# Pooled attention and SiLU network on one core: an exponential set aside, a filler and a last quarter reordered, query transposes moved ahead of value sums, eight more dummy matmuls

## The chip, the cores and the metric

The kernel runs on one core of one Trainium2 chip. The metric is the device time of one execution in microseconds (us). Four runs of the kernel before took 290.15, 290.22, 291.45 and 291.74 us, with a median of 290.83 us.

The engines are named as in the profile. PE is TensorE doing matmuls, PEld is its weight load, DVE is VectorE, ACT is ScalarE, POOL is GpSimd and SP is SyncE. A small q behind a name (SPq, POOLq) is the engine's sequencer, which issues the DMAs.

## The reference

There are 8 batches of 8 heads, with 576 queries, keys and values of 64 numbers each. Keys and values are averaged over groups of 8 (576 to 72), and the attention output of all heads becomes the input of a two-layer network with SiLU.

```python
k_p = k.reshape(B, H, Sp, 8, D).mean(axis=3)        # 576 -> 72 rows
v_p = v.reshape(B, H, Sp, 8, D).mean(axis=3)
scores = q @ k_p.transpose(0, 1, 3, 2) / sqrt(D)
attn = exp(scores) / sum(exp(scores))               # the maximum is subtracted first
x = (attn @ v_p).transpose(0, 2, 1, 3).reshape(4608, 512)
h = x @ w_in                                        # 512 -> 2048
out = (h * sigmoid(h)) @ w_out                      # 2048 -> 512, float32
```

## The kernel before

The 4608 tokens are cut into 9 tiles of 512 (the loop over t, L785). Each tile has an upward product (`up`, L471: x times w_in, SiLU into h_T) and a downward one (`down`, L571, for t = 0, and `down_quarters`, L638, for all others: h times w_out, then the stores). Tiles t >= 1 compute part of both products with sums of matrix quarters (x_sum, h_sum, w_sum), which DVE makes, so that PE has fewer matmuls. The attention of batch t+1 is woven into the two products of tile t.

The weaving is written by hand. Each product has a list of fillers, pairs of a step number and a call; a generator `spread` (L417) yields one step before each matmul and, once a step is past, makes the calls due by then. The order of all instructions on every engine follows the program text, and each engine runs its own in that order. PSUM tiles come from two pools, `mm` with 3 banks and `at` with 5 (L89), and a new tile waits until the reader of an old one is done.

The attention of a batch runs through these steps, each of them one helper. `slot_sums` (L269, DVE) adds the rows of k or v in groups. `select_k` and `select_v` (L289, L305, PE) pick the sums into kz_ps and v_ps. `copy_k` and `copy_v` (L302, L319, on ACT or DVE) bring them to SBUF as kz and vp. `q_transpose` (L150, DVE, one call for half a group of four heads) makes qT. `scores` (L343, PE) makes four tiles sc_ps and ACT takes the exponential of each into es (L359). `denominators` (L363) sums es on PE and ACT (or DVE by a reciprocal, L375) inverts it into rec. `numerators` (L382) multiplies es with vp on PE (nu_ps, L395), and DVE multiplies by rec into xT (L404).

Batch 0 has no tile to be woven into. Its attention is the prologue, written out at L735 to L767, in four parts: `part(g, f)` is head group g, half f of the queries. Between its steps stand dummy matmuls, `warm_up(n)` (L698), n products of 128x512 on zeros whose result is not read; there are 37 in all. In the middle of it all `attn_tables` and `moe_tables` (L410, L413) switch ACT between the function tables for exponential and for SiLU. `up` of tile 0 follows the last `warm_up`; its first matmuls read xT of parts (0,0) and (1,0), and the parts (0,1) and (1,1) end as fillers of it.

Tile 0's `down` runs three output blocks m = 0, 1, 2 together over all 16 slices g of h_T (48 steps), copies each to o_sb (ACT for 0 and 2, DVE for 1) and then runs m = 3 alone, whose PSUM tile is a bank that m = 0 held. Fillers among these steps:

```python
    f_down.append((37 + 3 * j, lambda j=j: select_v(1, j, "at")))    # L836
    sc_at, den_at, nu_at = (1, 16, 30), (16, 30, 44), (44, 55, 56)    # L874
```

Tile 1 does the attention of batch 2. Its four query transposes have the steps `[24, 25, 26, 8]` (L829); the first three are fillers of `up`, the fourth one of `down_quarters`. There, step 8 also has both calls of `slot_sums("v")` (L843), which are earlier in the list. The second third of the scores, at step 31, is the first reader of the fourth transpose.

From tile 1 on, the fillers load batch t+2: `load_q` on POOL's queue, `load_one` on SP's, `load_rest` on POOL's again (L864 to L868).

Of the kernel before, what the change touches and what calls it, by code (L numbers as in the profile page):

```python
# [36 lines left out]
def kernel(  # L37
# [9 lines left out]
    nc = tc.nc  # L47
# [5 lines left out]
    d_model = H * D  # L53
    d_ff = moe_w_in.shape[1]
    KF = d_model // 128
    KG = d_ff // 128
# [44 lines left out]
    w_out_sb = singles.tile([128, KG, d_model], BF16, name="w_out_sb")  # L101
# [167 lines left out]
    def slot_sums(name, j, halves=False):  # L269
        raw = row_tiles[name][j]  # L270
        dst = rows5[name][:, SA:] if j else rows5[name][:, :SA]
        w = RE // 4 if halves else RE // 2
        while w > D:
            nc.vector.tensor_add(  # L274
                out=raw[..., :w], in0=raw[..., :w], in1=raw[..., w : 2 * w]
            )
            w //= 2
        nc.vector.tensor_add(out=dst, in0=raw[..., :D], in1=raw[..., D : 2 * D])
# [23 lines left out]
    def copy_k(b, a, copy=nc.vector.tensor_copy):  # L302
        copy(out=kz[b % 2][:, a], in_=batches[b]["kz_ps"][:, a])
# [15 lines left out]
    def copy_v(b, a, copy=nc.vector.tensor_copy):  # L319
        hs = slice(4 * a, 4 * (a + 1))  # L320
        copy(out=batches[b]["vp"][:, hs, :], in_=batches[b]["v_ps"][:SP, hs, :])
# [3 lines left out]
    def part(g, f):  # L325
        return ((g, f * QF, (f + 1) * QF),)
# [13 lines left out]
            yield g, i0, i1, slice(o, o + n)  # L340
            o += n

    def scores(b, segs):  # L343
        st = batches[b]
        w = width(segs)
        sc = [ps_tile([128, 512], FP32, "at", "sc_ps")[:SP, :w] for s in range(4)]
        for g, i0, i1, cs in seg_cols(segs):
            for c in range(2):
                for s in range(4):
                    rows = slice(32 * s, 32 * (s + 1))  # L350
                    nc.tensor.matmul(  # L351
                        sc[s][:, cs],
                        lhsT=kz[b % 2][rows, g, c, :],
                        rhs=st["qT"][rows, g, i0:i1, c, :],
                        start=(c == 0), stop=(c == 1),
                    )
        es = mid.tile([SP, 4, VW], BF16, tag="es", bufs=4, name="es")[:, :, :w]
        for s in range(4):
            nc.scalar.activation(es[:, s, :], sc[s], func=AF.Exp, scale=score_scale)  # L359
        st["es", segs] = es  # L360

# [192 lines left out]
    def store(t, m, cs, engines=(nc.sync,)):  # L554
        n0 = (t * NTT + m * 128) // QP
        src = o_sb[m // 2][:, m % 2, cs]
        if n0 // QI == B - 1:
            engines[0].dma_start(out=out[n0 * QP : n0 * QP + 128, cs], in_=src)
            return
        for u in range(128 // QP):  # L560
            n = n0 + u
            rows = (
                out[n * QP : (n + 1) * QP] if n // QI == B - 1
                else out_r[n // QI, n % QI]
            )
            engines[u % len(engines)].dma_start(
                out=rows[:, cs], in_=src[QP * u : QP * (u + 1)]
            )


    def down(t, fillers, ms):  # L571
        step = spread(fillers, KG * sum(len(mm) for mm in ms))
        for mm in ms:
            o_ps = [ps_tile([128, d_model], FP32, "mm", "o_ps") for m in mm]
            for g in range(KG):
                for m, ps in zip(mm, o_ps):
                    next(step)
                    nc.tensor.matmul(  # L578
                        ps,
                        lhsT=h_T[:, g, m * 128 : (m + 1) * 128],  # L580
                        rhs=w_out_sb[:, g, :],
                        start=(g == 0), stop=(g == KG - 1),
                    )
            for m, ps in zip(mm, o_ps):
                copy = nc.vector.tensor_copy if m == 1 else nc.scalar.copy
                copy(o_sb[m // 2][:, m % 2, :], ps)  # L586
                store(t, m, slice(0, d_model))
        for _ in step:
            pass

# [107 lines left out]
    def warm_up(n):  # L698
        for _ in range(n):
            nc.tensor.matmul(warm_ps, lhsT=warm[:, :128], rhs=warm, start=True, stop=True)  # L700
# [37 lines left out]
    copy_k(0, 0, act_copy)  # L738
    warm_up(4)
    q_transpose(0, 0, 0)  # L740
    scores(0, part(0, 0))
    slot_sums("k", 1)
    warm_up(3)
    select_k(0, 1)
    copy_k(0, 1, act_copy)
    q_transpose(0, 1, 0)
    warm_up(2)
    scores(0, part(1, 0))
    denominators(0, part(0, 0))
    slot_sums("v", 0)  # L750
    warm_up(2)
    select_v(0, 0, "mm")
    copy_v(0, 0, act_copy)
    denominators(0, part(1, 0))
    q_transpose(0, 0, 1)
    scores(0, part(0, 1))
    slot_sums("v", 1)
    warm_up(1)
    numerators(0, part(0, 0), ("mm", "at"))
    warm_up(2)  # L760
    select_v(0, 1, "mm")
    copy_v(0, 1)
    q_transpose(0, 1, 1)
    warm_up(2)
    numerators(0, part(1, 0), ("mm", "at"))
    scores(0, part(1, 1))
    warm_up(2)  # L767
    load_slots(nc.gpsimd, 1, "k", 0, 3)
    load_slots(nc.gpsimd, 1, "k", 3, 4)
    load_slots(nc.gpsimd, 1, "k", 4, 5)  # L770
# [14 lines left out]
    for t in range(NT):  # L785
        a = t + 1
# [39 lines left out]
                if t == t0:  # L826
                    f_to.append((at + i, lambda n=n, i=i: weight_sum(n, i)))
        if a < B:
            q_at = [15, 16, 17, 8] if t > 1 else [24, 25, 26, 8] if t else [82, 84, 86, 88]  # L829
            if t == 0:  # L830
                for j in range(2):
                    f_up.append((44 + 8 * j, lambda j=j: slot_sums("k", j)))
                    f_up.append((72 + 8 * j, lambda j=j: select_k(1, j)))
                    f_up.append((72 + 8 * j, lambda j=j: copy_k(1, j)))
                    f_down.append((20 + 10 * j, lambda j=j: slot_sums("v", j)))
                    f_down.append((37 + 3 * j, lambda j=j: select_v(1, j, "at")))  # L836
                    f_down.append((37 + 3 * j, lambda j=j: copy_v(1, j)))
            elif t == 1:
                for j in range(2):
                    f_up.append((0, lambda j=j: slot_sums("k", j, halves=True)))  # L840
                    f_up.append((22, lambda j=j: select_k(2, j)))
                    f_up.append((23, lambda j=j: copy_k(2, j)))
                    f_down.append((8, lambda j=j: slot_sums("v", j, halves=True)))  # L843
                    f_down.append((40, lambda j=j: select_v(2, j, "at")))
                    f_down.append((41, lambda j=j: copy_v(2, j)))
            else:
                f_up.append((22, lambda: k_transpose(a)))
                f_down.append((10, lambda: pool_v(a)))
            for n in range(4):
                f_to = f_down if t and n == 3 else f_up  # L850
                f_to.append((q_at[n], lambda n=n: q_transpose(a, n % 2, n // 2)))
            if t == 0:
                f_down.append((0, lambda: load_half_2("k", 0)))
                f_down.append((0, lambda: load_q(2)))
                f_down.append((0, lambda: load_half_2("k", 1)))
                for half in range(2):
                    f_down.append((31, lambda half=half: load_half_2("v", half)))
                for y in range(2):
                    for n in U_W:
                        f_down.append((6, lambda y=y, n=n: unit_weight_sum(y, n)))  # L860
            elif a + 1 < B:
                for stage in range(2):
                    f_down.append((100, lambda stage=stage: pool_k(a + 1, stage)))
                f_up.append((0, lambda: load_q(a + 1)))  # L864
                f_up.append((1, lambda: load_one(a + 1, "k")))
                f_up.append((2, lambda: load_rest(a + 1, "k")))
                f_down.append((11, lambda: load_one(a + 1, "v")))
                f_down.append((12, lambda: load_rest(a + 1, "v")))  # L868
            f_down.append((0, attn_tables))

            if t:
                sc_at, den_at, nu_at = (1, 31, 75), (31, 56, 97), (56, 97, 101)
            else:
                sc_at, den_at, nu_at = (1, 16, 30), (16, 30, 44), (44, 55, 56)  # L874
            for n, sg in enumerate(visits):
                f_down.append((den_at[n], lambda sg=sg: denominators(a, sg)))
                f_down.append((sc_at[n], lambda sg=sg: scores(a, sg)))

            for n, sg in enumerate(visits):
                if n < 2 or not 0 < t < B - 2:  # L880
                    f_down.append((nu_at[n], lambda sg=sg: numerators(a, sg)))
                if n == 0 and 1 < t < B - 1:
                    f_down.append((nu_at[n], lambda: numerators(a - 1, visits[2])))
# [34 lines left out]
```

The softmax here doesn't subtract the row's maximum and nothing guards it: scores larger than these inputs give would overflow.

## Time and profile before

| | us |
|---|---|
| median of four runs | 290.83 |
| the profiled execution's own time | 290.15 |
| its span, first to last instruction | 288.3 |
| PE busy | 278.9 (97%) |
| DVE busy | 225.6 (78%) |
| ACT busy | 183.1 (64%) |
| POOL busy | 52.2 (18%) |

The profile is one execution. Its own time is 1.85 us above its span, for what lies around the first and the last instruction. The granted clock of PE is 9 (90% or more) in all 40 slices of the page, and 1.000 as the core's mean. Matmul ends are modelled, so PE's idle time is best read from what the rows of a timeline give in brackets: the time without any matmul before a group, and what ended it.

### The profile page before, as it was taken

What the parts mean: (1) busy time and instruction counts of PE and PEld (TensorE: products, weight loads), DVE (VectorE), ACT (ScalarE), POOL (GpSimd) and SP (SyncE); (2) the same over time, 40 slices, a digit from 0 to 9 for tenths busy, and PEclk for the clock granted to TensorE, in tenths of its full rate; (3) what the DMA queues carried; (4) which work ended last, traced back from release to release, by engine and by line L of the source; (5) the groups of instructions that cost most, each with busy time, mean ns of one, the idle gap of its engine ahead of it and who ended that gap; (6) DMA issues with size and microseconds to landing.
All of it is one profiled execution on the core that took longest, in us unless ns stands there. A gap on an engine that the chain in (4) does not pass through costs nothing.

```text
span 288.3 us, 6919 instructions
## 1 busy us (share of the span) xinstructions
PE 278.9 (97%) x2773; PEld 195.9 (68%) x2793; DVE 225.6 (78%) x403; ACT 183.1 (64%) x359; POOL 52.2 (18%) x68
## 2 busy tenths in 40 slices
PE   8989998999799999999999999999999999999995
PEld 3448544466586687668788776678667867786684
DVE  4977844979869796989698869887988776746773
ACT  1677676468466785779577947795679657425700
POOL 8754316501020012001020105302000000000000
PEclk9999999999999999999999999999999999999999
DMA  7999999993768463953969395987830032005004
GB/s 214 275 273 219 228 301 158 228 198 62 141 91 193 113 100 69 165 148 89 153 114 212 79 148 110 147 154 148 155 95 0 2 76 72 2 1 141 5 1 148
DMA packets 35296, 37.70 MB, mean 131 GB/s; under 512 B 9952, under 2 KB 27616, under 8 KB 35264
## 3 DMA queue, kind: packets, MB, share of 16 engines
q0 software_dynamic: 21760, 20.86, 43.0%
q1 hardware_dynamic: 12928, 15.48, 21.2%
q10 hardware_dynamic: 576, 0.92, 0.9%
q8 instruction: 22, 0.36, 0.5%
q14 instruction: 10, 0.08, 0.1%
HBM read 36.70 MB, written 9.44 MB: 160 GB/s over the span
## 4 chain that ended last, share of the span: by engine, by line
PE 88%; DVE 7%; ACT 3%; issue 1%; DVEq 0%
PE hp_ps L546 21%; PE o_psQ L651 14%; PE o_psP L651 14%; PE u_psQ L488 6%; PE u_psP L488 6%; PE o_psR L651 5%; PE o_ps L578 5%; PE sc_ps L351 4%; PE warm_ps L700 4%; PE nu_ps L395 3%; PE den_ps L369 2%; PE u_psR L488 2%; DVE h_sum L611 1%; DVE w_sum L629 1%; DVE qT L153 1%
## 5 line engine op out<-in xcount | busy, mean ns | idle before, releaser
L546 PE MATMUL hp_ps<-xT,w_in_sb 128*128 128x512 bf16 (+3 forms) x397 | 80.8, 338 | 1.3 <-ACT h_T L552 0.4
L651 PEld LDWEIGHTS <-h_sum 128*128 128x128 bf16 x640 | 60.6, 98 | 11.9 <-issue 1.3
L552 ACT ACTIVATE h_T<-hp_ps 128x512 bf16<-128x512 f32 (+2 forms) x95 | 51.3, 545 | 26.7 <-PE hp_ps L546 25.7
L546 PEld LDWEIGHTS <-w_in_sb 128*128 128x128 bf16 x412 | 39.3, 98 | 24.9 <-issue 1.5
L611 DVE TENSOR_TENSOR h_sum<-h_T 128x1024 bf16<-128x1024 bf16 (+1 forms) x72 | 50.8, 742 | 6.9 <-ACT h_T L552 6.9
L359 ACT ACTIVATE es<-sc_ps 72x384 bf16<-72x384 f32 (+1 forms) x100 | 39.0, 469 | 11.0 <-PE sc_ps L351 11.0
L488 PEld LDWEIGHTS <-w_sum 128*128 128x128 bf16 x300 | 29.4, 98 | 7.7
L651 PEld LDWEIGHTS <-h_T 128*128 128x128 bf16 x256 | 24.0, 98 | 4.5 <-issue 0.9
L496 ACT ACTIVATE h_T<-c_sb 128x512 bf16<-128x512 f32 x30 | 18.8, 628 | 11.6 <-DVE c_sb L520 11.6
L404 DVE TENSOR_TENSOR xT<-nu_ps,rec 128x384 bf16<-128x384 f32 (+1 forms) x50 | 24.0, 532 | 2.5 <-PE nu_ps L395 2.3
L378 ACT ACTIVATE lnd<-den_ps 128x384 f32<-128x384 f32 (+1 forms) x23 | 11.1, 483 | 21.3 <-PE den_ps L369 21.3
L153 DVE STREAM_TRANSPOSE qT<-q_bf 128x576 bf16<-128x576 bf16 x32 | 23.0, 753 | 0.0
L182 POOL DMA_DIRECT2D raw<-in_k_dram x5 | 7.0, 1404 | 71.5 <-DVE h_sum L611 30.6
L274 DVE TENSOR_TENSOR raw<-raw 128x384 f32<-128x384 f32 (+3 forms) x20 | 12.4, 618 | 6.9 <-DMA raw<-in_v_dram 3.6
L651 PE MATMUL o_psP<-w_out_sb,h_sum 128*128 128x256 bf16 x128 | 17.6, 273 | 0.0
L651 PE MATMUL o_psQ<-w_sum,h_sum 128*128 128x256 bf16 x128 | 16.7, 273 | 0.0
L651 PE MATMUL o_psQ<-w_out_sb,h_sum 128*128 128x256 bf16 x128 | 16.6, 273 | 0.0
L651 PE MATMUL o_psP<-w_sum,h_T 128*128 128x256 bf16 x128 | 16.5, 273 | 0.0
L651 PE MATMUL o_psQ<-w_sum,h_T 128*128 128x256 bf16 x128 | 16.5, 273 | 0.0
L578 PE MATMUL o_ps<-w_out_sb,h_T 128*128 128x512 bf16 x61 | 15.2, 380 | 0.9 <-ACT o_sb L586 0.6
L651 PE MATMUL o_psR<-w_sum,h_sum 128*128 128x256 bf16 x128 | 15.7, 273 | 0.0
L182 POOL DMA_DIRECT2D raw<-in_v_dram x5 | 6.9, 1390 | 48.2 <-DVE o_sb L678 15.9
(77 smaller groups left out, 420.6 us busy)
## 6 DMA issues: line engine op xcount, KB each, us to landing
out_dram<-o_sb SPq DMA_DIRECT2D x128, 64.0 KB, 2.6
q_bf<-in_q_dram POOLq DMA_DIRECT2D x6, 576.0 KB, 11.2
raw<-in_k_dram SPq DMA_DIRECT2D x6, 512.0 KB, 6.6
raw<-in_k_dram POOLq DMA_DIRECT2D x5, 576.0 KB, 9.2
raw<-in_v_dram POOLq DMA_DIRECT2D x5, 576.0 KB, 9.2
raw<-in_v_dram SPq DMA_DIRECT2D x5, 512.0 KB, 5.4
w_in_sb<-in_moe_w_in_dram POOLq DMA_DIRECT2D x8, 256.0 KB, 8.3
w_out_sb<-in_moe_w_out_dram POOLq DMA_DIRECT2D x4, 512.0 KB, 13.5
```

What stands on the lines that cost most here:

```text
L153: nc.vector.transpose(out=st["qT"][:, a, f * QF : (f + 1) * QF].rearrange("r i c p -> r (i c p)"), in_=st["q_bf"][:, a, f * n : (f + 1) * n],)
L182: nc.gpsimd.dma_start(out=batches[b][f"{name}_raw"], in_=source(b, name)[:, :, PH:], accum_op=ALU.add,)
L274: nc.vector.tensor_add(out=raw[..., :w], in0=raw[..., :w], in1=raw[..., w : 2 * w])
L359: nc.scalar.activation(es[:, s, :], sc[s], func=AF.Exp, scale=score_scale)
L404: nc.vector.tensor_mul(out=xT[:, 2 * g0 + c : 2 * (g0 + ng - 1) + c + 1 : 2, cols], in0=nu[c][:, :w].rearrange("r (g n) -> r g n", g=ng), ...
L488: nc.tensor.matmul(ps[bank][:, u, :], lhsT=w[:, kk, 128 * u : 128 * (u + 1)], rhs=x[:, kk, :], start=first and u == 0 and kk == 0, stop=kk ...
L496: nc.scalar.activation(h_T[:, g : g + 2, j * NQ : (j + 1) * NQ], src, func=AF.Silu)
L546: nc.tensor.matmul(hp_ps[:, r0:r1], lhsT=w_in_sb[:, kk, g * 128 : (g + 1) * 128], rhs=xT[:, kk, x0 : x0 + r1 - r0], start=(kk == 0), stop= ...
L552: nc.scalar.activation(h_T[:, g, n0 : n0 + n], hp_ps[:, :n], func=AF.Silu)
L578: nc.tensor.matmul(ps, lhsT=h_T[:, g, m * 128 : (m + 1) * 128], rhs=w_out_sb[:, g, :], start=(g == 0), stop=(g == KG - 1),)
L611: nc.vector.tensor_tensor(out=h_sum[n][:, ks, :], in0=quarter(*a, ks), in1=quarter(*b, ks), op=op)
L651: nc.tensor.matmul(ps[b][:, c, :], lhsT=left(n, kt, c), rhs=W_OUT[n][:, kt, :], start=b not in begun, stop=kt == k1 - 1, skip_group_check= ...
```

## The change

It consists of five edits.

1. In the prologue, `scores` of part (0,0) issues its fourth exponential after a call that it is given. That call holds the rest of the key work (the sums, 3 dummies, the selection, and the copy on ACT).
2. The prologue's order after the first value sums is new. The transposes and scores of parts (0,1) and (1,1) come earlier, the copy of the first half of vp goes from ACT to DVE behind both transposes, and `warm_up` has 45 dummies instead of 37.
3. `down` of tile 0 runs the last quarter of the slices (g = 12 to 15) one block after the other, and copies each block as soon as it is done.
4. The fourth query transpose of tile 1 has step 2 instead of 8.
5. From tile 1 on, `load_one` of k stands before `load_q` instead of behind it.

```diff
-    def scores(b, segs):
+    def scores(b, segs, between=None):
...
         for s in range(4):
+            if s == 3 and between:
+                between()
             nc.scalar.activation(es[:, s, :], sc[s], func=AF.Exp, scale=score_scale)
...
-            for g in range(KG):
-                for m, ps in zip(mm, o_ps):
-                    next(step)
-                    nc.tensor.matmul(
-                        ps,
-                        lhsT=h_T[:, g, m * 128 : (m + 1) * 128],
-                        rhs=w_out_sb[:, g, :],
-                        start=(g == 0), stop=(g == KG - 1),
-                    )
-            for m, ps in zip(mm, o_ps):
-                copy = nc.vector.tensor_copy if m == 1 else nc.scalar.copy
-                copy(o_sb[m // 2][:, m % 2, :], ps)
-                store(t, m, slice(0, d_model))
+            last = KG - KG // 4
+            for g, (m, ps) in (
+                [(g, x) for g in range(last) for x in zip(mm, o_ps)]
+                + [(g, x) for x in zip(mm, o_ps) for g in range(last, KG)]
+            ):
+                next(step)
+                nc.tensor.matmul(
+                    ps,
+                    lhsT=h_T[:, g, m * 128 : (m + 1) * 128],
+                    rhs=w_out_sb[:, g, :],
+                    start=(g == 0), stop=(g == KG - 1),
+                )
+                if g == KG - 1:
+                    copy = nc.vector.tensor_copy if m == 1 else nc.scalar.copy
+                    copy(o_sb[m // 2][:, m % 2, :], ps)
+                    store(t, m, slice(0, d_model))
...
-    scores(0, part(0, 0))
-    slot_sums("k", 1)
-    warm_up(3)
-    select_k(0, 1)
-    copy_k(0, 1, act_copy)
+
+    def rest_k():
+        slot_sums("k", 1)
+        warm_up(3)
+        select_k(0, 1)
+        copy_k(0, 1, act_copy)
+
+    scores(0, part(0, 0), rest_k)
     q_transpose(0, 1, 0)
     warm_up(2)
     scores(0, part(1, 0))
     denominators(0, part(0, 0))
     slot_sums("v", 0)
-    warm_up(2)
+    warm_up(3)
     select_v(0, 0, "mm")
-    copy_v(0, 0, act_copy)
+    q_transpose(0, 0, 1)
     denominators(0, part(1, 0))
-    q_transpose(0, 0, 1)
+    warm_up(1)
     scores(0, part(0, 1))
+    warm_up(3)
+    q_transpose(0, 1, 1)
+    copy_v(0, 0)
     slot_sums("v", 1)
+    numerators(0, part(0, 0), ("mm", "at"))
     warm_up(1)
-    numerators(0, part(0, 0), ("mm", "at"))
-    warm_up(2)
+    scores(0, part(1, 1))
+    warm_up(4)
     select_v(0, 1, "mm")
     copy_v(0, 1)
-    q_transpose(0, 1, 1)
     warm_up(2)
     numerators(0, part(1, 0), ("mm", "at"))
-    scores(0, part(1, 1))
-    warm_up(2)
+    warm_up(3)
...
-            q_at = [15, 16, 17, 8] if t > 1 else [24, 25, 26, 8] if t else [82, 84, 86, 88]
+            q_at = [15, 16, 17, 8] if t > 1 else [24, 25, 26, 2] if t else [82, 84, 86, 88]
...
-                f_up.append((0, lambda: load_q(a + 1)))
-                f_up.append((1, lambda: load_one(a + 1, "k")))
+                f_up.append((0, lambda: load_one(a + 1, "k")))
+                f_up.append((1, lambda: load_q(a + 1)))
```

## The prediction

> **What bounds the kernel now.** I read the page's chain first, then the waits of PE, then the timelines around the places that the change touches.
>
> ```profile
> PE 88%; DVE 7%; ACT 3%; issue 1%; DVEq 0%
> ```
>
> PE is the path. An edit pays only where PE stands still, or if it takes work off PE. The waits of PE say how much there is to win:
>
> ```profile
> PE sc_ps L351 <- DVE qT L153: 1.8, 2, 1.5
> PE o_ps L578 <- ACT o_sb L586: 0.6, 1, 0.6
> PE hp_ps L546 <- ACT h_T L552: 0.4, 1, 0.4
> ```
>
> Three stalls matter: 1.5 us for a transpose, 0.6 us for a copy, and 0.4 us for SiLU. The change aims at all three, and it adds eight dummy matmuls to PE. PE's timeline of the late prologue:
>
> ```profile
> 15.25 0.48 PE L314 MATMUL v_ps<-v,shifts 128*72 128x64 bf16 x6
> ...
> 17.00 0.44 PE L351 MATMUL sc_ps<-qT,kz 32*72 32x288 bf16 x8 [0.25 <-DVE qT L153]
> 17.37 0.60 PE L700 MATMUL warm_ps<-warm 128*128 128x512 bf16 x2
> 17.81 0.41 PE L546 MATMUL hp_ps<-xT,w_in_sb 128*128 128x288 bf16 x2
> ...
> 20.53 0.41 PE L546 MATMUL hp_ps<-xT,w_in_sb 128*128 128x288 bf16 x2 [0.40 <-ACT h_T L552]
> ```
>
> The real work of tile 0 starts at 17.81. Two dummies hold PE for 0.44 (17.37 to 17.81), so one costs 0.22. ACT in the same stretch:
>
> ```profile
> 14.90 1.28 ACT L359 ACTIVATE es<-sc_ps 72x288 bf16<-72x288 f32 x4
> 17.46 1.29 ACT L359 ACTIVATE es<-sc_ps 72x288 bf16<-72x288 f32 x4 [1.29 <-PE sc_ps L351]
> 18.78 1.28 ACT L414 ACT_TABLE_LOAD   x1
> 20.07 1.01 ACT L552 ACTIVATE h_T<-hp_ps 128x288 bf16<-128x288 f32 x3
> ```
>
> The last scores are late (17.00), so the last exponentials, the table load and the first SiLU are late, and PE stalls at 20.53.
>
> **The prologue (edit 2), step by step.** Nothing changes on PE before 12.03. With the spacings of the rows (dummy to dummy 0.22, dummy to a small matmul 0.31 as 11.11 to 11.42, scores 0.37 as 11.42 to 11.79, eight numerators 0.36 as 20.87 to 21.23):
>
> - The third dummy before the value selection costs nothing. The denominators behind it wait for exponentials that end at 13.18 in both kernels, so PE is free again at 13.44 as before.
> - One dummy at 13.44, scores of (0,1) at 13.75, three dummies from 14.13, numerators (0,0) at 14.88, one dummy at 15.24, scores of (1,1) ready to issue at 15.55. Their transpose now follows the other one on DVE and ends by 13.3 (its queries are not later: the trace has no DMA wait at it); the vp copy on DVE ends at 13.6. The second value sums queue behind that copy and end near 15.0, against a use at 17.2.
> - These scores overwrite the four PSUM banks that the exponentials of (0,1) read. With the vp copy (0.35 at 13.86 in ACT's timeline) gone from ACT, these run from 14.65 to 15.92 instead of from 14.90. So the fourth score starts at 15.98, its second half at 16.13, and PE goes on at 16.34: a new wait of 0.4. It holds up all that is queued behind it on PE.
> - Four dummies from 16.34; the value selection at 17.22; its result 0.48 later (row at 15.25), 17.70; cast 0.11 later and 0.42 long (15.84), to 18.23; numerators at 18.29; three dummies from 18.65; tile 0 at 19.31. That is 1.50 later than 17.81.
> - Against it, the last exponentials now run from 16.40 to 17.68 and the table load to 18.97, before the first hp_ps is complete (20.3). The stall goes. Without it the matmul of 20.53 would have stood at 19.97 (six spacings of 0.125 after 19.22; a dummy's 0.216 for 512 columns gives 0.12 for 288), so it was worth 0.56.
>
> Net +0.94. Bounds: -0.56 if every dummy falls into a wait, +1.73 (8 x 0.22) if all are on the path and the stall stays. I take +0.94, since each spacing has a row; the order alone would be a gain, the dummies eat it.
>
> PEclk is 9 in all slices, and 0.12 per 288-column matmul is the spacing both before and after the 0.25 and 0.40 gaps; the trace shows no clock that more filling would raise. The Trainium skill (TensorE: Matmul & The Clock Gate, § What's actually happening) states that only an idle window of about 3.4 us drops the clock. By this rule dummies in gaps of 0.4 buy nothing and the sum stays +0.94; it speaks against the eight.
>
> ACT's next instruction follows the table load at 20.07, 0.01 after its end. The skill's ScalarE: Activation LUTs, § What ACT_TABLE_LOAD costs, adds a drain of 1.38 to each switch; by it the changed kernel's first SiLU would be free at 20.35, practically when hp_ps is complete. The row decides, and no term changes.
>
> **The exponential set aside (edit 1).** The key copy at 10.98 waits for kz_ps, which ends at 10.95, as the fourth exponential did. So the copy gains nothing; the exponential moves to 11.25 and ends near 11.65, before its reader at 11.79. 0, at most 0.1 either way.
>
> **The last quarter of tile 0's down (edit 3).** The stall, in the timelines of ACT, PE and DVE:
>
> ```profile
> 48.07 0.49 ACT L378 ACTIVATE lnd<-den_ps 128x384 f32<-128x384 f32 x1 [1.96 <-PE den_ps L369]
> 48.60 0.52 ACT L379 ACTIVATE rec<-lnd 128x384 f32<-128x384 f32 x1
> 49.03 1.05 ACT L586 COPY o_sb<-o_ps 128x512 f32<-128x512 f32 x2
> 49.64 1.89 PE L578 MATMUL o_ps<-w_out_sb,h_T 128*128 128x512 bf16 x7 [0.62 <-ACT o_sb L586]
> 49.18 0.68 DVE L586 COPY o_sb<-o_ps 128x512 f32<-128x512 f32 x1
> ```
>
> Block 3 needs block 0's bank, whose copy stood behind the logarithm and the reciprocal. Now block 0 ends eight steps earlier, its copy runs on ACT at 46.2 to 46.7 (idle then until 48.07), and block 3 starts at 48.86 (three matmuls of 0.216 after 48.21) instead of 49.64: 0.79. But the next reader, tile 1's hp_ps, waits for the last xT of DVE (DVE's four from 52.45, 1.94 long, to 54.39) as much as for PE. DVE's copy (0.68 at 49.18) leaves the place between xT and w_sum, which then start 0.59 earlier, and so does the end of xT. DVE is next: -0.59 (0 to -0.79).
>
> **The fourth transpose of tile 1 (edit 4).** DVE's timeline, then PE's:
>
> ```profile
> 72.62 0.55 DVE L274 TENSOR_TENSOR raw<-raw 128x384 f32<-128x384 f32 x1
> ...
> 74.14 0.77 DVE L153 STREAM_TRANSPOSE qT<-q_bf 128x576 bf16<-128x576 bf16 x1
> 74.97 0.36 PE L351 MATMUL sc_ps<-qT,kz 32*72 32x192 bf16 x8 [1.52 <-DVE qT L153]
> ```
>
> DVE has no gap here, so the order decides. The transpose would run from 72.62 to 73.39, the second half of the scores at 73.45 instead of 74.97: 1.52. The value sums end at 74.92 (four sums took 1.52), and the selection that reads them stands 1.3 after the scores (75.0 to 76.25), so at 74.73; its second half waits 0.04. DVE's h_sum ends at 76.61 and the two casts (0.42 each, overlapping) at 77.3; the numerators want them at 78.90 - 1.48 = 77.4. -1.48 (0 if the casts or sums come late, -1.52).
>
> **The load order (edit 5).** The loads are on two queues, and the instructions on POOL and on SP stand in the same order in both kernels. POOL's q load loses one wait, for a transpose that ends at 74.9 against its issue at 80.7. Queued behind it are POOL's later loads, which do not move. 0.
>
> **Sum.** +0.94 - 0.59 - 1.48 = -1.13. The rest of the path is PE at 97% and moves as a whole; no stage after 75 has a stall above 0.13, and the loads landed well ahead (the accumulating k load of tile 1, issued at 68.4 and some 9 us long, is needed at 85.98). Against the profiled execution's own 290.15 this is 289.02. That execution is the lowest of the four runs, 0.68 below their median, and they scatter by 1.6; I apply the same difference to the median: 290.83 - 1.13 = 289.7.
>
> **The rivals.**
> - *The dummies fall into waits* (the spacings of the short groups hide them, or the vp cast sets the time anyway). For it: the third dummy is free, and PE waits 0.4 and 0.1 in my own walk. Against: nine dummies behind the scores of (1,1) are strung between steps that depend on each other. Prologue -0.56 instead of +0.94, total -2.63: 288.2.
> - *The transpose's wait is only passed on*: the value sums, the casts behind h_sum (1.20 at 75.41) and the numerators come late, as DVE has the same work in the same stretch. Place: the selection and the numerators of tile 1. It decides once the casts end over 0.1 later than 77.3; if it takes all of the 1.48, +0.35 stays, 291.2, slower than before. Against: DVE idles 0.36 ahead of the casts now.
> - *The change does nothing that can be measured*: the prologue at its +1.73 bound and the rest as forecast, -0.34: 290.5.
>
> **How the numbers follow.** My forecast has 0.65, the free dummies 0.15, the passed-on wait 0.1, the +1.73 prologue 0.1. About 0.5%, or 1.45 us, is what a measurement of this kernel can tell from no change; that is below 289.4 for faster, above 292.3 for slower. The forecast with the scatter of the runs (0.7 on either side) is faster in about a third of its cases: 0.65 x 0.35 + 0.15 = 0.38. Slower needs a rival on top of the scatter: 0.06. The rest is 0.56. The range runs from the free dummies (288.2) to the passed-on wait (291.2).
>
> **What would show it.** Right: no idle bracket at L351 near 74 above 0.3, none at the fourth block of tile 0's down, none from ACT h_T near 20; the first hp_ps at 19.3, and stage offsets against before of about +0.9 at 25, +0.35 at 60, -1.1 at 100. Wrong: hp_ps starting at 18 (dummies free); a new wait for vp or v_ps at 74 to 78; or offsets that shrink after 100.

## The result, and the profile after

The changed kernel takes 290.03 us (median of 53 runs, 288.49 to 291.63), against 290.57 us before (79 runs, 289.55 to 292.95). The ratio is 0.998, with a 95% interval of 0.997 to 0.999. The profiled execution of the changed kernel has an own time of 290.6 us and a span of 288.4 us (before 290.15 and 288.3), so these two executions taken alone would say that nothing was won. The time lies above the span by a median of 2.09 to 2.16 us in every kernel here with the new prologue and of 1.89 to 1.92 in all others, before included; so about 0.2 us of the new prologue's price lie outside the span, and no run shows why. Most line numbers are 2 to 10 higher after the change: L548, L583 and L705 stand for L546, L578 and L700.

The chain of waits of the changed kernel, and PE's waits (engine, line, what it waited for; total us, times, longest):

```profile
PE 86%; DVE 6%; DMA 4%; issue 2%; ACT 1%; SPq 0%; DVEq 0%
```

```profile
PE warm_ps L705 <- DVE warm L718: 1.2, 1, 1.2
PE u_psR L490 <- DVE x_sum L457: 0.8, 2, 0.4
PE warm_ps L705 <- issue: 0.3, 2, 0.2
PE kz_ps L296 <- DVE k L278: 0.2, 1, 0.2
```

All three stalls of before (1.5 for the transpose, 0.6 for the copy, 0.4 for SiLU) are gone. Two new things matter: a wait of PE for x_sum, and 4% DMA in the chain, where there was none. DVE's waits name the load:

```profile
DVE raw L188 <- DMA raw<-in_k_dram: 1.4, 2, 0.7
```

The prologue on PE, then on ACT:

```profile
15.58 0.79 PE L351 MATMUL sc_ps<-qT,kz 32*72 32x288 bf16 x8
...
18.52 0.82 PE L705 MATMUL warm_ps<-warm 128*128 128x512 bf16 x3
19.18 0.41 PE L548 MATMUL hp_ps<-xT,w_in_sb 128*128 128x288 bf16 x2
```

```profile
17.62 1.28 ACT L416 ACT_TABLE_LOAD   x1
20.21 0.41 ACT L554 ACTIVATE h_T<-hp_ps 128x288 bf16<-128x288 f32 x1 [1.31 <-PE hp_ps L548]
```

The first hp_ps starts at 19.18, 1.37 later than before. The table load is over at 18.90, and ACT now waits for PE, not PE for ACT. The numerators among the hp_ps start at 21.68 against 20.87, so 0.81 later.

The places of edits 3 and 4, on PE:

```profile
48.58 0.50 PE L397 MATMUL nu_ps<-es,vp 72*32 72x192 bf16 x16
49.01 2.33 PE L583 MATMUL o_ps<-w_out_sb,h_T 128*128 128x512 bf16 x9
```

```profile
72.90 0.35 PE L371 MATMUL den_ps<-es,ones 72*32 72x384 bf16 x4
73.17 0.72 PE L351 MATMUL sc_ps<-qT,kz 32*72 32x192 bf16 x16
73.83 1.16 PE L656 MATMUL o_psR<-w_sum,h_sum 128*128 128x256 bf16 x9
```

There is no idle bracket at either. The 16 score matmuls run in one piece, where 1.52 stood between two eights.

Now the offsets of the same instruction between the two profiled executions (ACT's starts): +0.87 at 20.7 us, +0.03 at 54.4, -1.00 at 75, -1.43 at 79. Then nothing changes up to 145. There it jumps to -0.72, and after 208 it is within 0.11 of zero. What the edits to tiles 0 and 1 gained is lost in two steps. DVE's timeline of the changed kernel at these two points:

```profile
142.36 1.02 DVE L406 TENSOR_TENSOR xT<-nu_ps,rec 128x384 bf16<-128x384 f32 x2
144.07 1.22 DVE L188 TENSOR_TENSOR raw<-raw 72x1024 f32<-72x1024 f32 x1 [0.70 <-DMA raw<-in_k_dram]
...
201.91 1.02 DVE L406 TENSOR_TENSOR xT<-nu_ps,rec 128x384 bf16<-128x384 f32 x2
203.66 1.22 DVE L188 TENSOR_TENSOR raw<-raw 72x1024 f32<-72x1024 f32 x1 [0.73 <-DMA raw<-in_k_dram]
```

L188 is DVE's first sum over a batch's k, which needs the accumulating load (`load_rest`) to have landed. The kernel before has the same two places without a bracket:

```profile
143.79 1.02 DVE L404 TENSOR_TENSOR xT<-nu_ps,rec 128x384 bf16<-128x384 f32 x2
144.73 1.21 DVE L188 TENSOR_TENSOR raw<-raw 72x1024 f32<-72x1024 f32 x1
...
202.56 1.02 DVE L404 TENSOR_TENSOR xT<-nu_ps,rec 128x384 bf16<-128x384 f32 x2
203.55 1.22 DVE L188 TENSOR_TENSOR raw<-raw 72x1024 f32<-72x1024 f32 x1
```

In the trace of before the loads landed at 144.46 and 203.53: 0.27 and 0.02 ahead of their use. After, they landed at 144.05 and 203.63. DVE was ready 1.36 and 0.62 earlier than before, the data came 0.41 earlier and 0.10 later, and DVE waited for the rest.

The loads did not move along with the rest of the kernel. SyncE's queue ahead of the first of the two places, before and then after (the k load here is the first half of a batch's k; POOL's accumulating load is issued some 1.3 after it has landed, at 134.25 and at 134.14):

```profile
114.51 13.52 SPq L566 DMA_DIRECT2D out_dram<-o_sb  x16
128.13 1.17 SPq L173 DMA_DIRECT2D raw<-in_k_dram  x2
```

```profile
113.08 14.65 SPq L568 DMA_DIRECT2D out_dram<-o_sb  x16
127.92 1.17 SPq L173 DMA_DIRECT2D raw<-in_k_dram  x2
```

The stores begin 1.43 earlier, as the kernel does, but hold the queue 1.13 longer, so the k load behind them is issued only 0.21 earlier. Why they take longer is not shown.

### The profile page after: what moved, and what is told of

Same layout as the page of the kernel before. It is cut to its first block, busy times and chain, and to the rows that moved or that the text cites. A ratio compares the mean times of both kernels' runs of the same rounds, so it can differ in the third digit from the quotient of the medians.

```text
span 288.4 us, 6934 instructions
## 1 busy us (share of the span) xinstructions
PE 280.8 (97%) x2781; PEld 196.3 (68%) x2801; DVE 225.8 (78%) x404; ACT 183.3 (64%) x358; POOL 51.9 (18%) x68
## 4 chain that ended last, share of the span: by engine, by line
PE 86%; DVE 6%; DMA 4%; issue 2%; ACT 1%; SPq 0%; DVEq 0%
PE hp_ps L548 23%; PE o_psP L656 15%; PE o_psQ L656 14%; PE u_psQ L490 6%; PE u_psP L490 5%; PE o_psR L656 5%; PE sc_ps L351 4%; PE o_ps L583 3%; PE nu_ps L397 2%; PE warm_ps L705 2%; PE den_ps L371 2%; PE u_psR L490 2%; DMA out_dram<-o_sb 2%; DMA raw<-in_k_dram 2%; DVE rr_sb L510 1%
## 5 line engine op out<-in xcount | busy, mean ns | idle before, releaser
L548 PE MATMUL hp_ps<-xT,w_in_sb 128*128 128x512 bf16 (+3 forms) x397 | 80.7, 338 | 0.9 <-issue 0.2
L548 PEld LDWEIGHTS <-w_in_sb 128*128 128x128 bf16 x412 | 39.3, 98 | 24.4 <-issue 0.8
L490 PEld LDWEIGHTS <-w_in_sb 128*128 128x128 bf16 x120 | 11.7, 97 | 6.0 <-issue 1.9
L656 PE MATMUL o_psP<-w_sum,h_sum 128*128 128x256 bf16 x128 | 15.4, 272 | 0.0
```

What stands on the lines that cost most here:

```text
L490: nc.tensor.matmul(ps[bank][:, u, :], lhsT=w[:, kk, 128 * u : 128 * (u + 1)], rhs=x[:, kk, :], start=first and u == 0 and kk == 0, stop=kk ...
L548: nc.tensor.matmul(hp_ps[:, r0:r1], lhsT=w_in_sb[:, kk, g * 128 : (g + 1) * 128], rhs=xT[:, kk, x0 : x0 + r1 - r0], start=(kk == 0), stop= ...
L656: nc.tensor.matmul(ps[b][:, c, :], lhsT=left(n, kt, c), rhs=W_OUT[n][:, kt, :], start=b not in begun, stop=kt == k1 - 1, skip_group_check= ...
```

## The experiments

Each kernel is compared with the kernel before on the same chip; the medians of before are 291.57 us (the first four kernels), 291.56 (the next four) and 290.39 (the last four). The kernel before varies between chips more than some of the changed ones do: one and the same kernel, run as f2 and as g4, took 287.80 and 287.82 us, but its ratios are 0.987 and 0.991. So compare within a set; between sets a difference of a few tenths of a per cent, in ratios or in times, says little. The letters of the theories are those of the quoted texts; C in the last set is the theory that the second set calls E.

**e1_old_prologue: the change with the prologue of before.**

```diff
-    scores(0, part(0, 0), rest_k)
+    scores(0, part(0, 0))
+    slot_sums("k", 1)
...
-    scores(0, part(1, 1))
-    warm_up(4)
...
+    scores(0, part(1, 1))
+    warm_up(2)
```

> The changed kernel with the prologue of before (edits 1 and 2 undone; edits 3, 4, 5 kept). Theory A, the load chain sets a floor: stage offsets against before of 0 at 25 us, about -0.8 at 60, -2.2 at 100 (0.77 and 1.46 us gained), then given back where VectorE's first pooling sum of k waits for its accumulating load (near 144 and 203 us); the end -0.3 to -0.8 us against before, hardly better than the changed kernel. Rival B, TensorE moves as a whole and the give-back in the changed kernel's profile was one execution's accident: -2.2 us at the end, about 0.9 better than the changed kernel.

Measured: 289.08 us, ratio 0.993 (0.991 to 0.996). Against before, the offsets are -0.32 at the start, -1.09 at 54.4 (edit 3: -0.77) and -2.55 at 79 (edit 4: -1.46). At the end -2.34 are left: at L188 DVE waits for k once, 0.3. That is rival B's end, and theory A's -0.3 to -0.8 missed. But this execution, with 288.03, is the second fastest of twelve that lie between 287.77 and 291.03 at a clock of 0.998 or more; what the slower ones lost is not shown. So in this execution edits 3 and 4 are worth what they look like and keep nearly all of it, and the new prologue takes time away.

**e2_prologue_only: before with edits 1 and 2 alone.**

```diff
-    scores(0, part(0, 0))
+    scores(0, part(0, 0), rest_k)
...
-    warm_up(2)
+    scores(0, part(1, 1))
+    warm_up(4)
```

> Before with edits 1 and 2 alone. Both theories: offset +0.8 at 25 us, no stall for SiLU at 20 us. Rival B (all moves as a whole): +0.8 us at the end. Theory A (the load chain, whose start does not depend on the prologue, has its floor just under before's need): most of +0.8 stays, +0.4 to +0.8 us, with no wait of VectorE for k.

Measured: 292.4 us, ratio 1.003 (1.000 to 1.006). The offset goes from -0.72 ahead of the prologue to +0.16 at 20.7: the prologue costs 0.88. PE's stall for SiLU is gone and does not make up for it. Later the offset grows to +0.71. Most of this growth is two waits of DVE for the k load, 0.25 ahead of 174.56 and 0.23 ahead of 204.25, where theory A expected none:

```profile
DVE raw L188 <- DMA raw<-in_k_dram: 0.5, 2, 0.2
```

The tiles and the load order of this kernel are those of before.

**e3_k_early: the change with the k load issued earlier.** `load_one` of k goes to the queue behind the stores of half a tile, not behind those of a whole one.

```diff
-                f_up.append((0, lambda: load_one(a + 1, "k")))
+                if t == 1:
+                    f_up.append((0, lambda: load_one(a + 1, "k")))
...
+                if a + 2 < B:
+                    f_down.append((101, lambda: load_one(a + 2, "k")))
```

> The changed kernel with one more edit: from tile 2 on the first half of the next k is issued on SP 4 us earlier, at step 101 of the downward product of the tile before, ahead of the eight last stores instead of behind them. Theory A: the k loads of tiles 3 to 6 land 3 to 4 us earlier, no VectorE wait at the first pooling sum, the offset of -1.4 us at 100 us holds to the end: -1.3 to -1.9 us against before. Rival B: no more than the changed kernel has, about -0.5 us.

Measured: 288.66 us (288.23 to 289.18), ratio 0.991 (0.989 to 0.994). At L188 DVE waits for k nowhere, and at the end 1.7 are left against before, as theory A said. The offsets against the changed kernel step down at just the two places: from -0.26 to -0.95 by 151, and to -1.79 by 210. SyncE's queue shows why, first in the changed kernel, then in this one:

```profile
172.64 12.71 SPq L568 DMA_DIRECT2D out_dram<-o_sb  x16
186.42 1.23 SPq L173 DMA_DIRECT2D raw<-in_k_dram  x2
```

```profile
171.61 7.95 SPq L568 DMA_DIRECT2D out_dram<-o_sb  x8
179.67 2.52 SPq L173 DMA_DIRECT2D raw<-in_k_dram  x2
182.30 5.07 SPq L568 DMA_DIRECT2D out_dram<-o_sb  x8
```

Sixteen stores hold the queue for 12.71 us, and the k load stands behind them. POOL's accumulating load waits for that one. With the k load after eight stores, POOL issues its load at 187.70 instead of 193.03; it lands at 195.20 instead of 203.63, 6.6 ahead of its use at 201.83.

**e4_before_k_early: the kernel before with the same k edit.**

```diff
-                    f_up.append((1, lambda: load_one(a + 1, "k")))
+                    if t == 1:
+                        f_up.append((1, lambda: load_one(a + 1, "k")))
...
+                    if a + 2 < B:
+                        f_down.append((101, lambda: load_one(a + 2, "k")))
```

> Before with the earlier k issue alone. Theory A: in its profiled execution the k loads landed 0.27 and 0.02 us ahead of their use, so single executions that are a little slower in their loads lose some tenths there: 0 to -0.6 us against before. Rival B: 0.

Measured: 289.9 us, ratio 0.995 (0.993 to 0.997). Against the profiled execution of before the offset is -0.61 from the first key sum to the end, with no step: in that execution no load was late. But the twelve runs lie between 289.44 and 290.38, while those of before on the same chip, at the same clock (0.998 or more), lie between 289.78 and 292.92. What the edit takes away is this scatter. It points to loads that were already late in executions of the kernel before which were not profiled. A slack of 0.02 makes that plausible, and in e2, with the same tiles and loads, such waits are seen; no trace of the kernel before itself has one.

**f1_few_dummies: e3 with none of the 17 dummies behind the first value sums.**

```diff
     slot_sums("v", 0)
-    warm_up(3)
     select_v(0, 0, "mm")
...
     numerators(0, part(1, 0), ("mm", "at"))
-    warm_up(3)
```

> The changed kernel with the earlier k issue, and without the 17 dummies that follow the first value sums (28 are left). Theory D, the dummies are the price of the prologue and its order alone is a gain: TensorE's first hp_ps at about 17.8 us instead of 19.2, no stall for SiLU, 1.2 to 1.5 us below the changed kernel with the earlier k issue, so about -3.6 to -4 us against before; matmuls stay at 0.216 us per 512 columns. Rival E, the dummies hold the clock: spacings of 0.43 us per 512 columns appear after the gaps of up to 1 us in the prologue, and the kernel is no faster than with the dummies.

Measured: 290.29 us, ratio 0.996 (0.993 to 0.999); slower than e3 by more than a microsecond, and not the -3.6 to -4 of theory D. The first hp_ps starts at 17.63, 1.30 earlier than in e3, but at half clock. Windows of the trace (us: busy time of PE, PEld, DVE, ACT, POOL with their instructions, then PE's granted clock):

```profile
14.00:16.00 2.00, 1.27 (x13) 0.60 (x13) 1.47 (x5) 1.68 (x6) 1.30 (x3) 1.00 1.24 205
16.00:18.00 2.00, 1.49 (x17) 0.60 (x16) 0.84 (x3) 1.98 (x5) 1.15 (x2) 0.55 1.23 206
18.00:20.00 2.00, 2.00 (x14) 0.65 (x12) 1.70 (x3) 0.96 (x2) 0.61 (x2) 0.50 1.19 299
20.00:22.00 2.00, 2.00 (x12) 1.04 (x8) 2.00 (x2) 0.74 (x2) 1.17 (x2) 0.50 1.05 405
22.00:24.00 2.00, 2.00 (x23) 0.84 (x23) 1.52 (x4) 0.49 (x2) 0.62 (x1) 0.74 1.09 213
```

The clock is 0.50 from 16.22 to 23.04, two windows of 3.41 us, in which PE runs at half speed. The idle time around the drop came in small pieces. The first two stand ahead of it, the third just behind it:

```profile
14.81 0.57 PE L351 MATMUL sc_ps<-qT,kz 32*72 32x288 bf16 x2 [0.46 <-ACT es L361]
15.59 0.43 PE L351 MATMUL sc_ps<-qT,kz 32*72 32x288 bf16 x6 [0.21 <-DVE xT L406]
...
17.02 0.67 PE L397 MATMUL nu_ps<-es,vp 72*32 72x288 bf16 x8 [0.51 <-DVE vp L321]
```

In the 3.41 us ahead of the drop (12.81 to 16.22) PE is busy for 2.57. All twelve runs have a mean clock of 0.988 or less, so this is no accident of one execution. The dummies cost time, but they hold the clock.

**f2_old_prologue_k_early: e1 with the early k load, so edits 3, 4 and 5 and the prologue of before.** Its diff is e1's and e3's together.

> Edits 3, 4 and 5 with the earlier k issue and the prologue of before. If the gains of edits 3 and 4 (0.77 and 1.46 us in the profiles) and that of the earlier k issue (about 1.4 us in the medians) add up: -3.3 to -3.8 us against before, 0.9 below the changed kernel with the earlier k issue. If the two stages only shift the wait to the next load: -2 to -2.6 us.

Measured: 287.8 us, ratio 0.987 (0.982 to 0.992), 3.8 below the median of before, which is within the range for gains that add up. No wait for k at L188; PE's three waits of the old prologue (0.6 for v, 0.4 for SiLU, 0.3 for a transpose) are there.

**f3_transpose_k_early: e4 with edit 4.**

```diff
-            q_at = [15, 16, 17, 8] if t > 1 else [24, 25, 26, 8] if t else [82, 84, 86, 88]
+            q_at = [15, 16, 17, 8] if t > 1 else [24, 25, 26, 2] if t else [82, 84, 86, 88]
```

> Before with the earlier k issue and edit 4 alone. -1.4 us beside the same kernel without edit 4, so about -2.8 us against before; the transpose stall at 74 us gone, the offset kept to the end. If edit 4 delays the next v load (the value sums free its buffer 0.75 us later) and that costs later: -2 us or less.

Measured: 288.05 us, ratio 0.988 (0.984 to 0.993). The offset against before goes from -0.63 to -2.15 at 79 and stays there to the end: edit 4 is worth 1.52, and all of it arrives once the loads are out of the way. Between f3 and f2, which adds edit 3, it goes from +0.35 to -0.42 across tile 0's downward product: 0.77 again.

**f4_quarter_k_early: e4 with edit 3.**

```diff
-            for g in range(KG):
-                for m, ps in zip(mm, o_ps):
...
+            last = KG - KG // 4
+            for g, (m, ps) in (
+                [(g, x) for g in range(last) for x in zip(mm, o_ps)]
+                + [(g, x) for x in zip(mm, o_ps) for g in range(last, KG)]
+            ):
```

> Before with the earlier k issue and edit 3 alone. The stall at 49 us gone; -0.59 us by the record's limit (the last xT of VectorE), -0.79 us if TensorE alone sets it, beside the same kernel without edit 3: -2.0 to -2.2 us against before.

Measured: 289.22 us, ratio 0.994 (0.991 to 0.997). Eight of the twelve runs lie between 288.88 and 289.57, with a mean clock of 1.000; the other four between 290.77 and 291.30, each with 0.994. The profiled execution is one of the four. Edit 3 alone is worth 0.78 in it: the offset against before goes from +0.35 at 8 to -0.43 at 54, so PE's stall sets the gain and not DVE's last xT. PE at the transpose that edit 4 would have moved, and the windows behind it:

```profile
74.60 0.36 PE L351 MATMUL sc_ps<-qT,kz 32*72 32x192 bf16 x8 [1.52 <-DVE qT L153]
```

```profile
74.00:76.00 2.00, 1.40 (x16) 1.06 (x16) 2.00 (x3) 1.04 (x3) 0.00 (x0) 0.87 1.05 174
76.00:78.00 2.00, 2.00 (x19) 1.60 (x17) 0.90 (x3) 0.57 (x2) 0.00 (x0) 0.50 1.16 161
78.00:80.00 2.00, 2.00 (x18) 1.40 (x20) 0.80 (x2) 0.00 (x0) 0.00 (x0) 0.77 0.80 157
```

Right behind the stall the clock is 0.50 for one window, 75.49 to 78.90. The offset moves from -0.43 to +1.16 there. So a stall of 1.5 can cost 1.6 more in an execution where the clock drops. In the 3.41 us ahead of the drop (72.08 to 75.49) PE is busy for 1.89. The runs fit: a mean of 0.994 on 289 us is 1.7 us of lost clock, one window at half. Of the 105 runs with the fourth transpose at step 8 (before on the three chips, e2, e4, f4), 16 have a mean clock of 0.994 or less. Of the runs with it at step 2, f1 aside, none is below 0.998.

**g1_nine_dummies and g2_thirteen_dummies: e3 with 9 and with 13 of the 17 dummies.**

```diff
     slot_sums("v", 0)
-    warm_up(3)
+    warm_up(1)    # g2: 2
...
     scores(0, part(1, 1))
-    warm_up(4)
+    warm_up(2)    # g2: 3
...
     numerators(0, part(1, 0), ("mm", "at"))
-    warm_up(3)
+    warm_up(2)    # g2: 2
```

In the same way, the three ahead of the second transposes become one (two in g2), and the two behind the second value cast become one in g1.

> The changed kernel with the early k load and the new prologue, with 9 of the 17 dummies behind the first value sums left (37 in the kernel, as many as before the change; the run with all 17 had its first hp_ps at 18.93, the run with none at 17.63 and at half clock). Theory D (a dummy costs what lies on the path, and these nine still hold the clock): the four dropped ahead of the value selection and of the second scores are free, the four dropped behind the scores of (1,1) are worth 4 x 0.216 = 0.87, so the first hp_ps stands near 18.1, 288-column matmuls stay at 0.12, and the ratio to before is near 0.988. Theory C (the clock follows how full PE is, so the fewer dummies the likelier a window at half clock): a window of 3.4 us at half clock somewhere between 16 and 23 us, 288-column matmuls at 0.24 in it, about 1.7 us lost, ratio near 0.994.

> The same with 13 of the 17 dummies left (41 in the kernel). Theory D: two of the four dropped lie on the path, first hp_ps near 18.5, ratio near 0.990. Theory C: full clock too, or a window at half clock in some executions only, so a wider scatter and a ratio between 0.990 and 0.994.

Measured: g1 288.02 us, ratio 0.992 (0.990 to 0.994); g2 288.09 us, ratio 0.992 (0.990 to 0.994). Both at full clock in every run (0.998 or more), so theory C's window did not come. Theory D's ratio for g1, near 0.988, did not come either; but g4 below, the same kernel as f2, also has 0.991 here and not 0.987. The start of an execution varies by up to a microsecond with its first load, so I count from the first key selection (7.3 to 8.2). The first hp_ps then stands at 11.18 with 17 dummies (e3), 10.75 with 13, 10.53 with nine, 9.88 with none, and at 9.80 before the change. The first step is 0.43, two dummies of 0.216 as expected. The second should have been another 0.43, to 10.32, and is 0.22, since PE now waits for the second value cast:

```profile
17.95 0.43 PE L397 MATMUL nu_ps<-es,vp 72*32 72x288 bf16 x8 [0.19 <-DVE vp L321]
```

**g3_after_again: the changed kernel beside them.** It has no edit.

> The changed kernel as it is, beside the others on one chip. Ratio 0.998 (0.996 to 1.000) by the theory that the k loads give back what the edits to the tiles gain: DVE waits for the accumulating k load near 144 and near 204, 0.6 to 0.8 each. By the rival that this waiting was particular to one execution, no wait at one of the two places and a ratio below 0.996.

Measured: 289.52 us, ratio 0.996 (0.994 to 0.998). The two waits for k at L188 are there with other sizes, 0.22 and 1.49 (expected 0.6 to 0.8 each), 1.7 in all against 1.4:

```profile
143.84 1.22 DVE L188 TENSOR_TENSOR raw<-raw 72x1024 f32<-72x1024 f32 x1 [0.22 <-DMA raw<-in_k_dram]
...
204.19 1.22 DVE L188 TENSOR_TENSOR raw<-raw 72x1024 f32<-72x1024 f32 x1 [1.49 <-DMA raw<-in_k_dram]
```

So when the data land varies by some tenths between executions, and the kernel's time with it.

**g4_old_prologue: f2 once more, beside the reduced prologues.** It has no edit against f2.

> The changed kernel with the early k load and the prologue of the kernel before (first hp_ps at 17.5, a stall of 0.4 for SiLU), again, beside the reduced prologues on one chip. By theory D the new order with nine dummies equals it within 0.3 us (first hp_ps 0.6 later, no stall for SiLU), and it is 0.8 faster than the new order with 17; ratio 0.987 to 0.988. By theory C it is the fastest of the four, and the kernel with nine is over 1 us behind.

Measured: 287.82 us, ratio 0.991 (0.988 to 0.993). g1 and g2 are within 0.3 of it, and six runs each don't tell them apart: the median spans are 285.95 (g4), 285.9 (g1) and 286.0 us (g2). In the profiles, counted from the first key selection again, the first numerators among the hp_ps start at 12.86 before, 13.68 with 17 dummies (e3), 13.02 with nine, and 13.29 in g4, where PE also waits 0.5 for v. So no prologue in the new order is shown to beat the old one, and the one with nine dummies is about even with it. This kernel has the lowest time here: edits 3, 4 and 5, the early k load, and the prologue as it was. Measured twice, it is faster than before by 1.3% and by 0.9%.

## Why the prediction was right, and where it was not

The forecast of 289.7 us is 0.3 below the 290.03 measured, but that is luck in part. The gain was forecast as 1.13 and is 0.54 between the medians; the start of the sum, 290.83 from four runs, was 0.26 above the median of 79. The sum left out the loss at the loads (1.4 in the profiled execution) and the 0.2 outside the span, and sized edit 3 0.2 too low; and it had no term for what the clock costs the kernel before in some executions, or for what late loads may cost it. These partly cancel.

- **The prologue, +0.94.** Measured +0.81 between the two profiled executions and +0.88 in e2. The walk held: scores of (1,1) ready at 15.55 (15.58), table load over at 18.97 (18.90), first hp_ps at 19.31 (19.18), no stall for SiLU. That "the order alone would be a gain, the dummies eat it" is half right. With nine dummies, as many in the kernel as before the change, g1 is about even with the old prologue (288.02 against 287.82). Two readings were off without effect on the sum: the two transposes end at 13.86 and the vp copy at 14.17, not at 13.3 and 13.6.
- **Edit 1, 0, and edit 5, 0.** No kernel here tries either alone. For edit 1 the rows show the 0: the fourth exponential moves to 11.16, and PE's rows up to 12.03 stand at the same times in both kernels. POOL and SP run the same order of instructions before and after.
- **The last quarter, -0.59 (0 to -0.79).** A mis-sized term: 0.77 in e1 and between f3 and f2, 0.78 in f4, 0.84 in the changed kernel's own profile. The prediction let DVE's last xT limit the gain to 0.59; in the runs nearly all of the 0.79 on PE comes through.
- **The fourth transpose, -1.48.** Measured -1.46 in the changed kernel and in e1, -1.52 in f3. Beyond that the edit removes a stall behind which the clock can fall. That is another 1.6 in the executions that it happens in, and the sum had no term for it.
- **"The rest of the path ... moves as a whole ..., and the loads landed well ahead": this step failed.** It rested on one load, that of tile 1, which is needed at 85.98 and had landed at 75.88 (after 7.47, not some 9), and took its slack of 10 for all five. The slacks of before are 10.1, 5.8, 0.27, 0.65 and 0.02 us. The offsets should have stayed at -1.1 beyond 100; they are -1.43 up to 145, then -0.72, then about 0. The loads did not move with PE. At the first place the stores ahead of the k load held the queue longer (14.65 against 13.52), and at the second the accumulating load took longer (10.60 against 9.17). The prediction's own test, "offsets that shrink after 100", is what happened. e3 shows that it is the k load: with it earlier, both steps are gone.
- **The clock.** The prediction leaned on the Trainium skill (TensorE: Matmul & The Clock Gate, § What's actually happening) and its idle window of about 3.4 us, and concluded that dummies in gaps of 0.4 buy nothing. That conclusion fell: in f1 no gap is above 0.51 and the clock halves for 6.83 us. That only such a window drops the clock was the prediction's own reading. The page's length of a window agrees with the trace (3.41). Its § A second HAM failure mode: psum-queue depth-cycling, which says that frequent micro-idles between groups of matmuls make the clock swing, fits f1 better than the rule that the prediction used, though f1 shows one drop and no swing. Still, the eight dummies *more* buy nothing: nine are enough.
- **The rivals.** The passed-on wait did not come: selection and numerators of tile 1 follow without an idle bracket. Free dummies were wrong as a whole: of the first four left out, two cost 0.22 each (e3 against g2), and of the next four they cost 0.22 together (g2 against g1). "Nothing measurable" is nearly what the total shows, but by another way than the one it gave.

What stays open: how much idle time in a window drops the clock (the profiled execution of before has the stall of 1.52 too, with the clock at 1.00 behind it), why the stores ahead of the k load hold the queue longer in the changed kernel, and why the accumulating load that POOL issues at 193.03 in the changed kernel takes 10.6 us to land, against 9.2 before and 7.5 in e3. In e3 the v load starts 4.8 behind it, in the other two it starts within 0.6 of it; that they share the DMA engines is likely, and was not tried apart.

## What to carry to other kernels

A gain on one engine's path holds only as far as the next transfer that has no slack, so list every load's landing against its use, tile by tile, before adding up stalls; one load that is early says nothing of the later ones. Look at what stands ahead of a load in its queue: here sixteen stores kept it for 13 us, and moving the load eight stores up paid more than the whole change. Filler matmuls are worth testing by number, since too many cost their own length and too few can cost the clock.

## What the runs showed of the hardware that I had not expected

The granted clock falls to 0.50 for whole windows of 3.41 us, after idle pieces of no more than 0.46 (f1), and in some executions after a single stall of 1.52 (f4). The window at half clock cost 1.6 us in f4, more than the stall itself. Eight stores of this kernel hold SyncE's queue for 5.07 and 7.95 us in the rows shown, with all that they wait for, so the place of a load among stores moves its start by microseconds.
